# Batch 3's mirrored transform rows from the banks of the others, residual rows gathered and output rows scattered by row number, in a new order

## Chip, core and metric

The kernel runs on one core of one Trainium2 chip. The metric is device time in microseconds of one execution. Engines are named as the profile does: PE (TensorE), DVE (VectorE), ACT (ScalarE), POOL (GpSimd) and SP (SyncE, which here only issues transfers).

## What is computed

A linear-attention recurrence over 768 steps for 4 batches and 8 heads of width 48, then per batch a two-dimensional Fourier mix, a normalisation and a two-layer feed-forward part:

```python
for t in range(S):                      # attention, state is 48 x 48 for each head
    y[:, :, t] = einsum('bhd,bhde->bhe', rt, state + u * kt (x) vt)
    state = wt[:, :, :, None] * state + einsum('bhd,bhe->bhde', kt, vt)
...
X = np.fft.fft(np.fft.fft(x, axis=1), axis=2)      # x: 4 x 768 x 384
u = x + np.real(X)
un = (u - mean(u)) / sqrt(var(u) + 1e-6)            # over the 384 columns
return u + maximum(un @ w_ch1, 0.0) @ w_ch2         # hidden width 1536
```

The real part of the transform of a real array has a symmetry: its value at row 768 - m and column (384 - d) mod 384 is its value at row m, column d.

## The kernel before

**Tiling.** A batch's 768 rows are six chunks (attention) or row blocks (mixing) of 128 rows on 128 partitions. For each chunk, four loads of 192 KB (w, k, r, v) are issued on SP into seven buffers each. The attention of a chunk takes a logarithm of w, two prefix matmuls (lines 773, 777), exponentials on ACT, products on DVE and POOL, two transposes (on PE, or for batch 3 as a DMA transpose on SP, line 819), a score group of sixteen matmuls (line 843), a masking on DVE (line 848), state matmuls (line 869) and the output matmuls (lines 896, 899), whose sum with the direct term becomes `x` (line 908). `fold` then adds and subtracts rows and columns of `x` so that the transforms work on symmetric halves.

**Mixing.** `mix(b)` runs once for each batch. Its steps:
- the row transform, 24 matmuls (line 968) into three banks, evicted to `hcs` (three parts j);
- from `hcs` a reversed copy `hcr` with signs, one operation for each j (lines 977 to 984), since the row blocks 3 to 5 of the transform are a mirror image of blocks 0 to 2;
- for each row block `kb` of six, three matmuls of 384 columns (line 992), against `hcs` for `kb` below 3 and against `hcr` from 3 on, into a bank of its own;
- a DVE sum of that bank with `x` into `uf`, with the row's sum (line 997), a centred copy `un` (line 1000) and a squared sum on ACT (line 1004);
- a transpose of three blocks' `un` into `unt` (for batches 2 and 3 a DMA transpose on SP, line 1033);
- for each half of three row blocks, twelve groups of three matmuls with W1 (line 1056), evicted with a ReLU to `ht` by ACT or DVE (lines 1062, 1064);
- for each row block twelve matmuls with W2 (line 1075, in three parts of four), a DVE operation that scales and adds `uf` into one of three output buffers `osb` (line 1081), and an output store on SP (line 1085). The very last row block is split into 256 and 128 columns.

**Order.** The program is recorded as a list of operations with what each reads and writes. Five hand-kept lists (`ORDER`) give the sequence of operation numbers on each engine. From these `schedule` gives out the eight PSUM banks and adds a few waits between DVE and POOL by a cost model with fixed durations; `emit` puts each engine's operations down in that sequence with the semaphore waits that remain. So the lists decide what stands ahead of what; every engine and SP's queue run in order. The weights are fetched by three transfers on POOL's queue (W1 in two halves, then W2), asked for in the middle of batch 0. Thirty-six filler matmuls (line 1130) stand in PE's list in the first part of the run, and sixteen before it (line 1098).

**Batch 3's end in the old order.** SP issues, after the last loads and the transposes of chunks (3,4) and (3,5), batch 2's outputs, the two `unt` transposes of batch 3 and the last outputs. PE's list runs batch 2's line 1056 and 1075 work between the last attention matmuls and batch 3's transforms.

Of the kernel before, what the change touches and what calls it, by code (L numbers as in the profile page):

```python
# [7 lines left out]
ALU = mybir.AluOpType  # L8
# [28 lines left out]
MEANS = (0, 1, 2, 3)  # L37
# [29 lines left out]
    "act": (  # L67
# [14 lines left out]
    "dve": (  # L82
# [14 lines left out]
    "pool": (  # L97
# [12 lines left out]
}  # L110


class _Tile:


    __slots__ = ("bank", "ops", "pool", "n_done", "end")
# [1047 lines left out]
```

## Time and profile before

| what | value |
|---|---|
| median of three runs | 183.61 us (183.61 to 183.76) |
| profiled execution, its own time | 184.21 us |
| span of that execution in the profile | 182.4 us |
| granted TensorE clock | 1.00 |
| DVE busy | 148.2 us in 341 instructions |
| ACT busy | 130.2 us in 340 |
| POOL busy | 101.5 us in 120 |
| bytes moved by DMA | 28.99 MB, mean 159 GB/s |
| loads of w, k, r and v | 24 each of 192 KB, 3.8 to 4.1 us from issue to landing (median) |

The span is the time between the first and the last instruction that the profile shows; the profiled execution's own time is 1.81 us longer. The page gives each engine's busy time as a share of the span; a chain followed back from the last instruction, from each step to what released it; and groups of instructions by line. Matmuls overlap in the array, so a matmul's own duration (its latency) is about twice what it costs in a row of them.

### The profile page before, as it was taken

The page shows a single profiled execution, that of the slowest core. Times are in us where ns is not written, and L with a number is a line of the kernel's source. Part 1 is how long each engine was busy: PE and PEld are TensorE (multiplying, and loading weights), DVE is VectorE, ACT ScalarE, POOL GpSimd, SP SyncE. Part 2 cuts the span into 40 slices and gives each one's busy share as a digit, 9 for nine tenths or more (in the row PEclk, how much of TensorE's full clock was granted, in tenths as well). Part 3 has the DMA queues.
Part 4 walks back from the last instruction along what each step waited for, and adds up shares of the span by engine and source line. Part 5 has one row for each costly group of instructions (what it writes and reads, how often), then busy time and mean ns, then how long its engine had stood idle before and what let it go on. Part 6 is the DMA issues. An engine that isn't in the chain of part 4 may idle for free.

```text
span 182.4 us, 4568 instructions
## 1 busy us (share of the span) xinstructions
PE 176.8 (97%) x1722; PEld 116.3 (64%) x1722; DVE 148.2 (81%) x341; ACT 130.2 (71%) x340; POOL 101.5 (56%) x120
## 2 busy tenths in 40 slices
PE   7999999999999999999999999999999999999994
PEld 3465676766566666776657666656666676666663
DVE  8779999899899999999888997899979927622343
ACT  2889859597898675799899978888882247478200
POOL 2448789767231498589998968769653440000000
DMA  4999998999999899999999999997550103331214
GB/s 97 203 216 196 208 191 172 185 202 208 152 196 190 162 210 230 226 204 182 202 222 218 219 177 207 220 212 179 103 114 0 47 2 65 73 125 43 86 71 145
DMA packets 116119, 28.99 MB, mean 159 GB/s; under 512 B 111361, under 2 KB 116098, under 8 KB 116098
## 3 DMA queue, kind: packets, MB, share of 16 engines
q1 hardware_dynamic: 114514, 26.36, 70.2%
q0 software_dynamic: 1584, 2.36, 8.0%
q8 instruction: 13, 0.21, 0.5%
q14 instruction: 8, 0.07, 0.1%
HBM read 23.59 MB, written 4.72 MB: 155 GB/s over the span
## 4 chain that ended last, share of the span: by engine, by line
PE 61%; DVE 17%; DMA 9%; SPq 4%; ACT 4%; issue 3%; DVEq 0%
PE bank L1075 18%; PE bank L1056 17%; DMA in_w<-in_w_dram 5%; DMA w<-in_moe_w_ch_dram 4%; DVE ah L848 4%; SPq L609 4%; PE bank L992 3%; PE bank L1130 3%; PE bank L1098 3%; PE bank L968 3%; DVE osb L1081 2%; PE bank L843 2%; DVE rkh L561 2%; PE bank L889 2%; PE bank L899 2%
## 5 line engine op out<-in xcount | busy, mean ns | idle before, releaser
L1075 PE MATMUL bank<-w,ht 128*128 128x384 bf16 (+2 forms) x300 | 53.7, 320 | 0.0
L1056 PE MATMUL bank<-unt,w 128*128 128x384 bf16 x288 | 51.9, 326 | 0.6 <-DMA w<-in_moe_w_ch_dram 0.6
L1064 ACT ACTIVATE ht<-bank 128x384 bf16<-128x384 f32 x72 | 32.6, 496 | 9.3 <-PE bank L1056 8.9
L1056 PEld LDWEIGHTS bank<-unt,w 128*128 128x128 bf16 x288 | 26.9, 98 | 17.5 <-DVE ht L1062 0.8
L1075 PEld LDWEIGHTS bank<-w,ht 128*128 128x128 bf16 x300 | 27.5, 98 | 15.2
L848 DVE TENSOR_TENSOR ah<-bank,msk 128x512 bf16<-128x512 f32 x48 | 31.2, 682 | 2.1 <-PE bank L843 2.0
L561 POOL TENSOR_TENSOR rk<-rk,ub 128x384 f32<-128x384 f32 x21 | 21.6, 1034 | 8.6 <-DVE rk L561 7.0
L561 POOL TENSOR_TENSOR vtd<-in_v,dc 128x384 f32<-128x384 f32 x20 | 16.7, 837 | 11.2 <-DVE dc L800 8.1
L1081 DVE SCALAR_TENSOR_TENSOR osb<-bank,rstd,uf 128x384 f32<-128x384 f32 (+2 forms) x25 | 14.8, 596 | 9.5 <-PE bank L1075 5.9
L1062 DVE TENSOR_SCALAR ht<-bank 128x384 bf16<-128x384 f32 x24 | 13.0, 549 | 6.9 <-PE bank L1056 6.8
L561 POOL TENSOR_TENSOR rk<-in_r,in_k 128x384 f32<-128x384 f32 x17 | 16.9, 999 | 2.9 <-DMA in_r<-in_r_dram 1.4
L997 DVE SCALAR_TENSOR_TENSOR uf<-bank,x 128x384 f32<-128x384 f32 x24 | 12.5, 553 | 4.7 <-PE bank L992 4.6
L561 POOL TENSOR_TENSOR rkh<-in_k,e 128x384 bf16<-128x384 f32 x14 | 14.1, 1009 | 3.6 <-ACT e L792 2.0
L779 ACT ACTIVATE bank<-bank 128x384 f32<-128x384 f32 x24 | 11.5, 484 | 5.8 <-PE bank L773 5.8
L811 DVE TENSOR_TENSOR rkh<-bank,in_r 128x384 bf16<-128x384 f32 x24 | 13.1, 549 | 2.1 <-ACT bank L779 2.0
L575 ACT ACTIVATE xf<-uf,agg 128x384 bf16<-128x384 f32 x24 | 14.7, 614 | 0.0
L561 POOL TENSOR_TENSOR xf<-sd 128x382 bf16<-128x382 f32 (+1 forms) x10 | 10.6, 1062 | 6.5 <-DVE sd L561 3.0
L575 ACT ACTIVATE lb<-in_w 128x384 bf16<-128x384 f32 x24 | 12.4, 519 | 2.1 <-DMA in_w<-in_w_dram 1.8
L575 ACT ACTIVATE un<-uf,agg 128x384 bf16<-128x384 f32 x18 | 10.6, 611 | 4.1 <-DVE uf L997 4.1
L586 ACT ACTIVATE rkt<-bank 128x256 f32<-128x256 f32 x29 | 10.8, 389 | 3.6 <-PE bank L833 2.4
L561 POOL TENSOR_TENSOR sd<-x 128x385 f32<-128x385 f32 x10 | 10.0, 1015 | 5.9 <-DVE x L908 5.4
L792 ACT ACTIVATE e<-bank 128x392 f32<-128x392 f32 (+1 forms) x24 | 11.7, 497 | 2.3 <-DVE bank L877 1.0
(138 smaller groups left out, 358.7 us busy)
## 6 DMA issues: line engine op xcount, KB each, us to landing
in_w<-in_w_dram SPq DMA_DIRECT2D x24, 192.0 KB, 3.8
in_k<-in_k_dram SPq DMA_DIRECT2D x24, 192.0 KB, 3.8
in_r<-in_r_dram SPq DMA_DIRECT2D x24, 192.0 KB, 4.1
in_v<-in_v_dram SPq DMA_DIRECT2D x24, 192.0 KB, 4.0
out_dram<-osb SPq DMA_DIRECT2D x23, 192.0 KB, 2.8
w<-in_moe_w_ch_dram POOLq DMA_DIRECT2D x2, 576.0 KB, 8.1
w<-in_moe_w_ch_dram POOLq DMA_DIRECT2D x1, 1152.0 KB, 10.7
out_dram<-osb SPq DMA_DIRECT2D x1, 128.0 KB, 1.7
```

What stands on the lines that cost most here:

```text
L561: return lambda e: e.tensor_tensor(out=o, in0=a, in1=b, op=f)
L575: return lambda e: e.activation(o, a, f, **kw)
L779: op("act", a_ps(DM) + 20, lambda e: e.activation(ps(tce)[:, 0:DM], ps(tce)[:, 0:DM], ACTF.Exp), w=[tce])
L792: op("act", a_ps(ne), lambda e: e.activation(E2[i2][:, 0:ne], ps(tci)[:, 0:ne], ACTF.Exp), r=[tci], w=[("E2", i2)])
L811: op("dve", v_1(DM), lambda e: e.tensor_tensor(out=rh[:, :, 0:D], in0=ps(tce)[:, 0:DM].rearrange("t (h d) -> t h d", d=D), in1=rt[:, :, :] ...
L848: masked[n] = op("dve", v_1(512), lambda e, x=x: e.tensor_tensor(out=ah[:, x:H:2, :], in0=ps(ta[x])[:, :].rearrange("p (h t) -> p h t", t= ...
L997: op("dve", v_1(DM) + 60, lambda e, kb=kb, t=t: e.scalar_tensor_tensor(out=uf[:, kb, :], in0=ps(t)[:, 0:DM], scalar=1.0, in1=xb[:, kb, 0:D ...
L1056: ins = e.matmul(ps(t)[:, 0:384], W1[:, m, 256 * (j // 2) + j % 2:256 * (j // 2) + 256:2], unt[:, :, m, :], start=(m == 0), stop=(m == NM ...
L1062: {"dve": lambda e, j=j, t=t, ht=ht: e.tensor_scalar(out=ht[:, j, :], in0=ps(t)[:, 0:384], scalar1=su, scalar2=0.0, op0=ALU.mult, op1=ALU. ...
L1064: "act": lambda e, j=j, t=t, ht=ht: e.activation(ht[:, j, :], ps(t)[:, 0:384], ACTF.Relu, scale=su)},
L1075: ins = e.matmul(ps(t)[:, 0:hi - lo], ht[:, j, 128 * x:128 * x + 128], W2[:, j, lo:hi], start=(j == 0), stop=(j == NJ - 1))
L1081: op("dve", v_1(hi - lo) + 64, lambda e, kb=kb, t=t, o=o, lo=lo, hi=hi: e.scalar_tensor_tensor(out=o[:, lo:hi], in0=ps(t)[:, 0:hi - lo], s ...
```

## The change

Batch 3 alone is mirrored (`MIRROR = (3,)`).

- No reversed copy `hcr` is made for batch 3. The banks of row blocks 0, 1 and 2 hold 385 columns instead of 384 (`DTM` has one more column, the first one repeated), and each serves two sums: the plain one for block `kb`, and one that reads the bank's columns 384 to 1 backwards for block `kb + 3`. Row block 3 + q then holds, on partition p, row 768 - (128 q + p), not row 384 + 128 q + p. Row 384 falls on partition 0 of block 3 and gets two matmuls with one output row and a DVE sum on one partition.
- The residual `x` for these rows has to stand on the same partitions. The chunks 3 to 5 of `x` are stored to an internal DRAM tensor by two transfers on SP, and three indirect transfers on POOL's queue gather the rows by number into `uf`.
- The output rows of these blocks are scattered by number: three indirect transfers on POOL's queue take the place of three output stores on SP. The end of the program waits for these too.
- The halves change places: in batch 3 the mirrored half goes first through the feed-forward part's buffers, and the split of the last row block moves to block 2.
- Two small index tables are made on POOL, with two one-element fills.
- The `BST` statistics buffers and the branch that used them, which no batch took, are gone.
- The cost model's load duration changes from 960 to 920 (batch 0) and 1030 (others), and all five lists of `ORDER` are new (left out here).

```diff
-MEANS = (0, 1, 2, 3)
+MIRROR = (3,)
...
-                if o.xfer == 960:
+                if o.xfer in (920, 1030):
...
-                    if s.startswith("out"):
+                    if s[:3] in ("out", "fin"):
...
+    XD = {b: nc.dram_tensor("xd%d" % b, (S // 2, DM), FP32, kind="Internal").ap() for b in MIRROR}
+    RIX = sb("rix", [NP], mybir.dt.uint32)
+    OIX = {b: sb("oix%d" % b, [NP], mybir.dt.uint32) for b in MIRROR}
...
-    DTM = sb("dtm", [3, DM], BF16)
+    DTM = sb("dtm", [3, DM + 2], BF16)
...
+    def move(fn, r, w, sem, xfer):
+        op("sp", 620, fn, r=r, w=w, sem=sem, xfer=xfer, dma=(1150, 600))
...
+    def places():
+        g.ctx = "places"
+        op("pool", 100, lambda e: e.iota(RIX[:, :], [[-128, NP]], base=S // 2, channel_multiplier=-1), w=["RIX"])
+        op(None, {"dve": 60, "pool": 100}, fill(RIX[0:1, 0:1], 0), w=["RIX"])
+        for b in MIRROR:
+            op("pool", 100, lambda e, b=b: e.iota(OIX[b][:, :], [[-128, NP]], base=S * (b + 1), channel_multiplier=-1), w=["OIX%d" % b])
+            op(None, {"dve": 60, "pool": 100}, fill(OIX[b][0:1, 0:1], S * b + S // 2), w=["OIX%d" % b])
...
+            if b in MIRROR:
+                continue
             sg = (1.0, CP[:, :], -1.0)[j]
...
+        if b in MIRROR:
+            xd = XD[b].rearrange("(c p) d -> p c d", p=128)
+            move(lambda e: e.dma_start(xd[:, 0:2, :], xb[:, 3:5, 0:DM]), [("X", i, 3), ("X", i, 4)], [("XD", b, 0)], "xa%d" % i, 1040)
+            move(lambda e: e.dma_start(xd[:, 2, :], xb[:, 5, 0:DM]), [("X", i, 5)], [("XD", b, 1)], "xb%d" % i, 520)
+            for q in (1, 2, 0):
+                op("pool", 1000, lambda e, q=q: e.indirect_dma_start(
+                    uf[:, NP + q, :], None, XD[b], bass.IndirectOffsetOnAxis(ap=RIX[:, q:q + 1], axis=0)),
+                   r=[("XD", b, 0), ("XD", b, 1), "RIX"], w=[("UF", i, NP + q)], sem="xz%d" % q, xfer=520, port=("pool",))
+        for kb in (0, 3, 1, 4, 2, 5) if b in MIRROR else range(NC):
...
+            flip = b in MIRROR and kb >= NP
+            if not flip:
+                t = made[kb] = g.tile("f")
+                for j in range(3):
+                    def f(e, j=j, kb=kb, t=t, w=DM + (b in MIRROR)):
...
+            t = made[kb % NP if flip else kb]
...
+            op("dve", v_1(DM) + 60, lambda e, kb=kb, t=t, flip=flip: e.scalar_tensor_tensor(
+                out=uf[:, kb, :], in0=ps(t)[:, DM:0:-1] if flip else ps(t)[:, 0:DM], scalar=1.0,
+                in1=uf[:, kb, :] if flip else xb[:, kb, 0:DM], op0=ALU.mult, op1=ALU.add,
+                accum_out=agg[:, kb, 0:1]), r=[t, ("UF" if flip else "X", i, kb)], w=[("UF", i, kb), ("SUM", i, kb)])
+            if flip and kb == NP:
...
+                        ins = e.matmul(ps(t)[0:1, 0:DM], hcs[:, j, DM:DM + 1], DTM[:, j, 0:DM], start=(j == 0), stop=(j == 1))
...
-        for hf in range(2):
-            q = 2 * b + hf
+        for hf in ((1, 0) if b in MIRROR else (0, 1)):
+            q = 2 * b + place[hf]
...
-                for lo, hi in ((0, DM),) if n < B * NC - 1 else ((0, 256), (256, DM)):
+                for lo, hi in ((0, DM),) if (b, hf, x) != (B - 1, 0 if b in MIRROR else 1, 2) else ((0, 256), (256, DM)):
...
+                    mq = kb - NP
+                    op("pool", 1000, lambda e, o=o, mq=mq: e.indirect_dma_start(
+                        out.rearrange("b s d -> (b s) d"), bass.IndirectOffsetOnAxis(ap=OIX[b][:, mq:mq + 1], axis=0), o[:, :], None),
+                       r=[("OSB", n % 3, 0), "OIX%d" % b], w=[("out", b, kb, 0)], sem="fin%d" % mq, xfer=520, port=("pool",))
```

In the new lists, PE's last work is row block 1 of batch 3, whole, with block 0 and the parts of the split block 2 just before it; the mirrored half's last part stands 5.9 us of matmuls ahead of the end. SP issues the two stores of `x` right behind the transpose of chunk (3,5), ahead of batch 1's last output. POOL's last six operations are the three gathers and the three scatters. The second half of W1 is asked for on POOL behind a product of chunk (1,2) and, by the wait that the cost model adds, behind DVE's reversed copy of batch 0.

More of the change, by code (lines that the diff above doesn't have):

```diff
@@ L492, in bass_rwkv6_finch__then__fnet_fourier_mix_kernel @@
     UF = [sb("uf%d" % i, [NC, DM], FP32) for i in range(2)]
-    BST = [sb("bst%d" % i, [6], FP32) for i in range(4)]
     AGG = [sb("agg%d" % i, [NC, 2], FP32) for i in range(2)]
@@ L610, in load_one @@
                                                 src[n][b, :, c * CH:(c + 1) * CH, :].rearrange("h t d -> t h d")),
-               w=[("in", n, i)], sem="in_%s%d" % (n, i), xfer=960)
+               w=[("in", n, i)], sem="in_%s%d" % (n, i), xfer=920 if b == 0 else 1030)
         loads[b, c, n] = o
         g.ctx = was
+    def move(fn, r, w, sem, xfer):
+        op("sp", 620, fn, r=r, w=w, sem=sem, xfer=xfer, dma=(1150, 600))
     def small(n, fn, **kw):
@@ L734, in rows @@
                         idn = (IDW if cos or half else NIDW)[p0:p0 + np_, 128 - sh:256 - sh]
-                        src = tab[:, 0:HE] if half == 0 else tab[:, HE - 2:0:-1]
-                        dst = ps(t)[:, 0:HE] if half == 0 else ps(t)[:, HE:DM]
+                        src = tab[:, 0:HE] if half == 0 else tab[:, HE - 2::-1]
+                        dst = ps(t)[:, 0:HE] if half == 0 else ps(t)[:, HE:DM + 1]
                         ins = e.matmul(dst, idn, src, start=(i == 0), stop=(i == len(moves[j]) - 1))
@@ L739, in tables_end @@
             op("pe", 900, rows, r=["IDB", "NIDW"] + [(n, q) for n in ("SS", "CS", "SSl", "CSl") for q in range(2)], w=[t])
-            op("act", a_ps(DM), lambda e, j=j, t=t: e.activation(DTM[:, j, :], ps(t)[:, 0:DM], ACTF.Copy), r=[t], w=["DTM%d" % j])
+            op("act", a_ps(DM), lambda e, j=j, t=t: e.activation(DTM[:, j, 0:DM + 1], ps(t)[:, 0:DM + 1], ACTF.Copy), r=[t], w=["DTM%d" % j])
     def weights():
@@ new lines, in mix @@
+        su = -1.0 / DM
+        made = {}
+        place = {x: 1 - x if b in MIRROR else x for x in range(2)}
+        if b in MIRROR:
[6 more added lines that the diff above has]
+                   r=[("XD", b, 0), ("XD", b, 1), "RIX"], w=[("UF", i, NP + q)], sem="xz%d" % q, xfer=520, port=("pool",))
@@ new lines, in mix, with f @@
+        for kb in (0, 3, 1, 4, 2, 5) if b in MIRROR else range(NC):
+            n = b * NC + kb
+            flip = b in MIRROR and kb >= NP
[3 more added lines that the diff above has]
+                    def f(e, j=j, kb=kb, t=t, w=DM + (b in MIRROR)):
+                        a = 128 * (kb % NP)
+                        return e.matmul(ps(t)[:, 0:w], (hcs if kb < NP else HCR)[:, j, a:a + 128], DTM[:, j, 0:w],
+                                        start=(j == 0), stop=(j == 2))
+                    op("pe", mm(DM), f, r=[("HCS" if kb < NP else "HCR", j), "DTM%d" % j], w=[t])
+            t = made[kb % NP if flip else kb]
+            iu = (2 * b + place[kb // 3]) % len(UN)
+            un = UN[iu][:, kb % 3, :]
+            op("dve", v_1(DM) + 60, lambda e, kb=kb, t=t, flip=flip: e.scalar_tensor_tensor(
[3 more added lines that the diff above has]
+            if flip and kb == NP:
+                t = g.tile("f")
+                def f(e, t=t):
+                    for j in range(2):
+                        ins = e.matmul(ps(t)[0:1, 0:DM], hcs[:, j, DM:DM + 1], DTM[:, j, 0:DM], start=(j == 0), stop=(j == 1))
+                    return ins
+                op("pe", mm(DM, 2), f, r=[("HCS", j) for j in range(2)] + ["DTM%d" % j for j in range(2)], w=[t])
+                op("dve", v_1(DM) + 60, lambda e, kb=kb, t=t: e.scalar_tensor_tensor(
+                    out=uf[0:1, kb, :], in0=ps(t)[0:1, 0:DM], scalar=1.0, in1=xb[0:1, kb, 0:DM], op0=ALU.mult, op1=ALU.add,
+                    accum_out=agg[0:1, kb, 0:1]), r=[t, ("X", i, kb)], w=[("UF", i, kb), ("SUM", i, kb)])
+            op(None, {"act": a_sb(DM) + 95, "dve": v_2(DM) + 60},
+               {"act": act(un, uf[:, kb, :], ACTF.Identity, scale=-float(DM), bias=agg[:, kb, 0:1]),
+                "dve": ts(un, uf[:, kb, :], -float(DM), agg[:, kb, 0:1], ALU.mult, ALU.add)}, port=("dve",),
+               r=[("UF", i, kb), ("SUM", i, kb)], w=[("UN", iu, kb % 3)])
+            op("act", a_sb(DM) + 190, act(xf[:, kb, 63:447], uf[:, kb, :], ACTF.Square, scale=-float(DM), bias=agg[:, kb, 0:1],
+                                          accum_out=agg[:, kb, 1:2]),
+               r=[("UF", i, kb), ("SUM", i, kb)], w=[("AGG", i, kb)] + [(z, i, kb) for z in ("XFe", "XFo", "XFn")])
@@ L1020, in mix @@
             hf = kb // 3
-            unt = UNT[(2 * b + hf) % 2]
+            unt = UNT[(2 * b + place[hf]) % 2]
             if b < DMA_U:
@@ L1030, in mix @@
                 evict(lambda kb=kb, unt=unt: unt[:, kb % 3, :, :].rearrange("p m t -> p (m t)"), lambda tu=tu: psb(tu)[:, 0:DM], DM, 2,
-                      r=[tu], w=[("UNT", (2 * b + hf) % 2, kb % 3)])
+                      r=[tu], w=[("UNT", (2 * b + place[hf]) % 2, kb % 3)])
             elif kb % 3 == 2:
@@ L1034, in mix @@
                     out=unt[:, :, :, :].rearrange("p x m t -> p (x m) t"), in_=UN[iu][:, :, :].rearrange("p x m -> p (x m)")),
-                   r=[("UN", iu, x) for x in range(3)], w=[("UNT", (2 * b + hf) % 2, x) for x in range(3)],
-                   sem="unt%d" % ((2 * b + hf) % 2), xfer=T_XFER, dma=T_LAT)
+                   r=[("UN", iu, x) for x in range(3)], w=[("UNT", (2 * b + place[hf]) % 2, x) for x in range(3)],
+                   sem="unt%d" % ((2 * b + place[hf]) % 2), xfer=T_XFER, dma=T_LAT)
             if kb % 3 == 2:
                 sl = slice(kb - 2, kb + 1)
-                if b in MEANS:
-                    op("act", 187, lambda e, sl=sl: e.activation(lnv[:, sl], agg[:, sl, 1], ACTF.Ln, bias=BEPS[:, :],
-                                                                 scale=float(DM) ** -3),
-                       r=["BEPS"] + [("AGG", i, x) for x in range(kb - 2, kb + 1)], w=[("LNV", i, hf)])
-                else:
-                    op("act", 187, lambda e, sl=sl: e.activation(lnv[:, sl], agg[:, sl, 1], ACTF.Ln, bias=BEPS[:, :]),
-                       r=["BEPS"] + [("AGG", i, x) for x in range(kb - 2, kb + 1)], w=[("LNV", i, hf)])
+                op("act", 187, lambda e, sl=sl: e.activation(lnv[:, sl], agg[:, sl, 1], ACTF.Ln, bias=BEPS[:, :],
+                                                             scale=float(DM) ** -3),
+                   r=["BEPS"] + [("AGG", i, x) for x in range(kb - 2, kb + 1)], w=[("LNV", i, hf)])
                 op("act", 95, lambda e, sl=sl: e.activation(rstd[:, sl], lnv[:, sl], ACTF.Exp, scale=-0.5),
                    r=[("LNV", i, hf)], w=[("RSTD", i, hf)])
-        for hf in range(2):
-            q = 2 * b + hf
+        for hf in ((1, 0) if b in MIRROR else (0, 1)):
+            q = 2 * b + place[hf]
             unt, ht = UNT[q % 2], HT[q % 2]
@@ L1084, in mix @@
                        r=[t, ("RSTD", i, hf), ("UF", i, kb)], w=[("OSB", n % 3, lo)] + ([] if lo else [("OSB", n % 3, 256)]))
-                    op("sp", 620, lambda e, kb=kb, o=o, lo=lo, hi=hi: e.dma_start(
-                        out[b, kb * 128:(kb + 1) * 128, lo:hi], o[:, lo:hi]),
-                       r=[("OSB", n % 3, lo)], w=[("out", b, kb, lo)], sem="out%d" % (n % 3), xfer=520, dma=(1150, 600))
+                    if b not in MIRROR or kb < NP:
+                        move(lambda e, kb=kb, o=o, lo=lo, hi=hi: e.dma_start(out[b, kb * 128:(kb + 1) * 128, lo:hi], o[:, lo:hi]),
+                             [("OSB", n % 3, lo)], [("out", b, kb, lo)], "out%d" % (n % 3), 520)
+                        continue
+                    mq = kb - NP
+                    op("pool", 1000, lambda e, o=o, mq=mq: e.indirect_dma_start(
+                        out.rearrange("b s d -> (b s) d"), bass.IndirectOffsetOnAxis(ap=OIX[b][:, mq:mq + 1], axis=0), o[:, :], None),
+                       r=[("OSB", n % 3, 0), "OIX%d" % b], w=[("out", b, kb, 0)], sem="fin%d" % mq, xfer=520, port=("pool",))
     g.ctx = "begin"
@@ L1103, in bass_rwkv6_finch__then__fnet_fourier_mix_kernel @@
     masks()
+    places()
     fills()
```

32 lines of the change are left out of this document (removed), and 128 rows, old and new, of the table ORDER.

## The prediction

> **What bounds the kernel now.** I read the page first, then who TensorE (PE) waited for, busy time by stretch, and the chain that ended last.
>
> ```profile
> span 182.4 us, 4568 instructions
> ...
> PE 61%; DVE 17%; DMA 9%; SPq 4%; ACT 4%; issue 3%; DVEq 0%
> ```
>
> PE carries most of the chain that set the end. The waits of PE (who waited for whom, us in total, times, longest) are few:
>
> ```profile
> PE bank L1098 <- DVE w L572: 1.3, 1, 1.3
> PE bank L1056 <- DMA w<-in_moe_w_ch_dram: 0.6, 1, 0.6
> PE bank L777 <- ACT ht L1064: 0.3, 1, 0.3
> PE bank L833 <- POOL rkh L561: 0.3, 1, 0.3
> PE bank L843 <- ACT ht L1064: 0.2, 1, 0.2
> ```
>
> These are all of them, 2.7 us. By stretch (its bounds and length, busy us and count of PE, PEld, DVE, ACT, POOL, then granted clock, DMA share, GB/s):
>
> ```profile
> 45.00:112.00 67.00, 65.89 (x735) 44.90 (x734) 63.05 (x129) 57.56 (x162) 47.40 (x51) 1.00 1.03 200
> 112.00:150.00 38.00, 37.84 (x350) 24.74 (x348) 31.18 (x68) 25.23 (x65) 23.73 (x26) 1.00 0.54 116
> 150.00:180.00 30.00, 29.81 (x196) 18.46 (x193) 13.57 (x33) 13.80 (x38) 0.34 (x1) 1.00 0.28 81
> ```
>
> Up to 112 us the loads keep the DMA engines full (share 1.03) and VectorE (DVE) is busy 63 of 67 us: PE, DVE and DMA are all near their limit. After 112 us the DMA share falls to 0.54 and 0.28 and only PE stays full. The chain agrees (start us, us, what):
>
> ```profile
> 37.82 8.02 DMA w<-in_moe_w_ch_dram
> 45.97 1.14 PE bank L1056 x6
> ...
> 112.59 0.40 PE bank L843 x8
> ...
> 136.87 0.55 PE bank L843 x16
> ...
> 156.38 7.80 PE bank L1056 x48
> ...
> 173.28 6.54 PE bank L1075 x52
> ...
> 179.92 0.35 DVE osb L1081
> ```
>
> From 112.59 us to 179.82 (173.28 + 6.54), the end of PE's work, the chain is PE and nothing else. In it 48 matmuls of 384 columns take 7.80 us, 0.1625 us each: my unit below. A score group (sixteen matmuls of line 843) takes 0.55 us.
>
> Is PE short of time before 112 us too? At 45.97 it starts the first matmul that needs the second half of W1. Counted in those two units, the matmuls that stand behind that point in the old order make about 131 us; the clock to 179.82 shows 133.9. So about 3 us of hidden gaps lie between 46 and 112 us, and there are the fillers (line 1130, 36 in either order) and the start before that. A new order can win back at most these; what it can lose has no such bound.
>
> **The change part by part.** On PE, batch 3's mixing loses nine matmuls that read the reversed copy `hcr` and gains two for row 384. In batch 3 what touches that copy is (smallest, median, largest ns, then first and last start):
>
> ```profile
> L992 PE MATMUL bank<-dtm,hcr x9: 326/326/326, 150.9 to 153.5; 128*128 128x384 bf16 x9
> L978 ACT ACTIVATE hcr<-hcs x2: 507/512/516, 149.3 to 151.0; 128x384 bf16<-128x384 bf16 x2
> L565 POOL TENSOR_SCALAR hcr<-hcs,cp x1: 1250/1250/1250, 149.1 to 149.1; 128x384 bf16<-128x384 bf16 x1
> ```
>
> The 326 ns is the latency of one; in a pipelined row it costs 0.1625 us. PE saves 7 x 0.1625 = 1.14 us, in a stretch where PE alone sets the end. The three copies (0.51, 0.51 and 1.25 us) go too, but they ran beside matmuls of line 1075 while PE never waited: worth nothing; were PE to run dry there, one copy's 0.51 us would be the gain. Widening the other matmuls by one column is 0.4 ns each: nothing.
>
> The end gets longer. The old order's last PE work is the 128-column part of the split last row block. In the new order the split block is x = 2 of the unmirrored half, but the last PE work is x = 1 of that half, unsplit: 384 columns to evict and 192 KB to store after PE's end. The rows for both sizes:
>
> ```profile
> 178.38 0.62 DVE L1081 SCALAR_TENSOR_TENSOR osb<-bank,rstd,uf 128x384 f32<-128x384 f32 x1 [0.68 <-PE bank L1075]
> ...
> 179.92 0.35 DVE L1081 SCALAR_TENSOR_TENSOR osb<-bank,rstd,uf 128x128 f32<-128x128 f32 x1 [0.19 <-PE bank L1075]
> ```
>
> ```profile
> out_dram<-osb SPq DMA_DIRECT2D x1, 192.0 KB, 1.9
> ...
> out_dram<-osb SPq DMA_DIRECT2D x1, 64.0 KB, 1.6
> ```
>
> That is 0.62 - 0.35 = 0.27 us on DVE and 1.9 - 1.6 = 0.3 us on the store, 0.57 us that nothing hides.
>
> The residual's way through DRAM (two stores on SP, three gathers on POOL) is new. It lies beside matmuls, so it costs nothing if it is in time. I count back from PE's end E by the matmuls behind each point in the new order. The attention products of chunks (3,4) and (3,5) have changed places: (3,5)'s now comes first and ends 40.3 us before E. These rows price the steps:
>
> ```profile
> 142.57 0.54 DVE L908 TENSOR_TENSOR x<-bank,vtd 128x384 f32<-128x384 f32 x1
> ...
> 149.92 0.56 DVE L997 SCALAR_TENSOR_TENSOR uf<-bank,x 128x384 f32<-128x384 f32 x1 [3.46 <-PE bank L992]
> ```
>
> ```profile
> w<-in_moe_w_ch_dram POOLq DMA_DIRECT2D x2, 576.0 KB, 8.1
> w<-in_moe_w_ch_dram POOLq DMA_DIRECT2D x1, 1152.0 KB, 10.7
> ```
>
> ```profile
> 37.82 0.80 POOL L745 DMA_DIRECT2D w<-in_moe_w_ch_dram  x1 [0.73 <-DVE rkh L561]
> 38.88 0.99 POOL L561 TENSOR_TENSOR rk<-in_r,in_k 128x384 f32<-128x384 f32 x1 [0.26 <-DVE hcr L565]
> ```
>
> ```profile
> unt<-un SPq DMA_TRANSPOSE x4, 3.3
> ```
>
> X of (3,5) is ready at E-39.6 (0.54 and a handover). The store, priced at the 1.9 us of an output store, lands by about E-37.3. Nothing in the trace is an indirect DMA. Its issue I take at 0.8 us, as POOL's weight DMA. Its landing is bounded by 1.9 us (192 KB from SP) and 10.7 us (1152 KB on POOL's queue, among loads); I take 3, near the low end, since its size is the former's and the DMA share there is 0.28 to 0.54. Issued at E-37.3, -36.5 and -35.7, the last lands at E-32.7. DVE comes to the first flipped sum only at about E-28.3: PE ends row block 0 at E-29.6, then follow DVE's sum of it (0.56) and an output eviction (0.62). So there are 4 us in hand. The three flipped sums and the one for row 384 end at about E-26.1, `un` at E-25.4, and its transpose (3.3 us) at E-22.1; PE needs it at E-20.5. The margin of the whole path is 1.6 us, and a gather must take 9 to 10 us before it fails. At the high bound of 10.7 us the sums start 2.6 us late and PE loses 1.0 us there.
>
> SP's queue holds, behind the second store of X, batch 1's last output, the transpose of the unmirrored half and two of batch 2's outputs; an output that waits there only holds its buffer, and batch 2 needs that buffer later, at E-27. The transpose is needed at E-24.1; its last `un` comes from row block 0, so it is asked at about E-28.2 and lands at E-24.9, 0.8 us in hand.
>
> The three scatters replace SP's outputs. The mirrored half comes first, its last row block leaves PE at E-5.9, is evicted at E-5.2 and issued on POOL, which has nothing else to do. It would have to take 8 us to land after the last plain output (E+2.7). At 10.7 us it would cost about 2.8 us; I take nothing.
>
> The index set-up (two iotas, two fills) is under 0.5 us on POOL and DVE in a start that has fillers on PE: nothing.
>
> The new order as such is the large unknown. Every queue changes. I found one place where the old order had PE wait on a transfer: the second half of W1, asked at 37.82 and needed 8.02 us later. The old order lets POOL ask for it behind a DVE product of chunk (1,2), the new one behind DVE's reversed copy in batch 0, which in the old order released POOL's next product only at 38.88. Behind the same first product of chunk (1,0), the new order has three operations ahead of that copy, the old one five. Bounds of the order's effect: the 3 us of hidden gaps gained, or a comparable amount lost; I take 0, since the amount of PE work ahead of that point differs by only 0.2 us in the two orders.
>
> Sum: -1.14 + 0.57 = -0.57 us. On the profiled span of 182.4 us that is 181.8; the profiled execution took 184.21 us, 1.81 around its span, so 183.64; the median shown is 0.60 under that execution: 183.04, given as 183.0.
>
> **The rivals.** (a) The second half of W1 comes later, and the kernel is slower. Place: POOL's ask in batch 0. For it: PE already waits 0.6 us there, so each us of delay goes through to the end, and DVE, which has to reach the copy first, is busy 63 of the next 67 us. Against: the copy has fewer operations ahead of it now. It decides as soon as the ask comes after 37.82; a copy at its old place gives 38.88 - 37.82 = 1.1 us: 183.04 + 1.1 = 184.1.
>
> (b) The gathers or scatters are late, as priced at the high bound: 183.04 + 1.0 to 2.8, middle 184.9. For it: POOL's queue shows 8.1 and 10.7 us. Against: those were larger transfers among loads.
>
> The Trainium skill, in SBUF — State Buffer, section "SBUF: two separate sides", says that a DMA issued from GpSimd has its descriptors written through a port that VectorE's two-port modes lock; this rule would make the late gathers of (b) likelier wherever DVE runs such an instruction beside them. By it the time would be that of (b), without it that of the forecast; no run so far shows an indirect DMA, so the trace does not decide it.
>
> (c) The new order also closes half of the hidden gaps: 183.04 - 1.5 = 181.5. For it: with DMA at 1.03 and DVE at 94% there, the order of loads matters. Against: the gaps are only 3 us in 66.
>
> **How the numbers follow.** Forecast 0.45, with its own range 182.5 to 183.6; (a) 0.25; (b) 0.10; (c) 0.20. A measurement of this kernel can tell about 0.2%, 0.37 us, from no change: faster is below 183.24, slower above 183.98. Of the forecast's 0.45, 0.28 lies below 183.24, 0.15 within and 0.02 above. So faster 0.28 + 0.20 = 0.48, same 0.15, slower 0.02 + 0.25 + 0.10 = 0.37. The range of 8 in 10 takes in most of (c) and of (a) and (b): 181.7 to 185.2.
>
> **What would show it.** Right: PE without a gap in the chain from about 112 us on, no wait of PE for `unt` of batch 3; the nine matmuls gone; span minus PE's end about 3.1 us where it was 2.6; gathers landing in about 3 us. Wrong: a wait of PE or of DVE on a gather, or a last landing from POOL's queue after SP's (b); a wait of PE for `w` well over 0.6 us (a); first transform matmuls of batch 3, seen from PE's end, where they stood, but PE's end more than 2 us earlier (c).

## The result and the profile after

The changed kernel takes 182.18 us (median of 20 runs), beside 183.61 us for the kernel before on the same chip (20 runs). The ratio is 0.9936 with an interval of 0.9913 to 0.9958: 1.2 us faster, from 0.8 to 1.6. It is taken without the slow executions of both kernels, so 1.2 us is not the difference of the two medians. The forecast was 0.57 us faster. A second comparison on another chip gave 0.9921 (0.9887 to 0.9956). The direction was right and the gain is about twice as large. The profiled execution took 182.78 us for a span of 181.0; before it was 184.21 and 182.4.

Read in the order of the prediction. First all waits of PE in the changed kernel (who waited for whom, us in total, times, longest):

```profile
PE bank L1126 <- DVE w L574: 1.3, 1, 1.3
PE bank L912 <- DVE ah L861: 1.3, 1, 1.3
PE bank L1159 <- DVE idw L567: 0.2, 1, 0.2
PE bank L902 <- POOL vtd L563: 0.2, 1, 0.2
PE bank L840 <- DVE rkh L824: 0.2, 1, 0.2
PE bank L882 <- ACT e L805: 0.2, 1, 0.2
```

No wait for `unt` and, in this execution, none for `w` from DRAM. By stretch, with the columns as before:

```profile
45.00:112.00 67.00, 67.00 (x747) 45.74 (x746) 63.13 (x133) 58.19 (x163) 44.45 (x48) 1.00 0.97 198
112.00:150.00 38.00, 38.00 (x352) 24.34 (x350) 34.05 (x75) 26.20 (x66) 27.01 (x28) 1.00 0.66 141
150.00:180.00 30.00, 27.85 (x184) 17.21 (x181) 15.42 (x33) 9.18 (x27) 2.97 (x3) 1.00 0.32 99
```

From 45 to 112 us PE is now busy in all 67.00 us, with 747 matmuls; before it was 65.89 and 735. So in this pair of profiles the change gained where the forecast had put a zero. In the last stretch PE is busy without a break up to its end at 177.7. The chain and VectorE (DVE) at the end:

```profile
165.63 3.25 PE bank L1098 x20
169.37 7.84 PE bank L1098 x60
```

```profile
174.41 0.48 DVE L1104 SCALAR_TENSOR_TENSOR osb<-bank,rstd,uf 128x256 f32<-128x256 f32 x1 [1.26 <-PE bank L1098]
176.66 0.35 DVE L1104 SCALAR_TENSOR_TENSOR osb<-bank,rstd,uf 128x128 f32<-128x128 f32 x1 [1.76 <-PE bank L1098]
177.31 1.27 DVE L1104 SCALAR_TENSOR_TENSOR osb<-bank,rstd,uf 128x384 f32<-128x384 f32 x2 [0.30 <-PE bank L1098]
```

The two small pieces of the split block are evicted first, and two full ones follow, as the diff showed. For the new way through DRAM, POOL's own instructions first (the first gather waits for the stores of x), and then transfers (count, KB each, median us to landing):

```profile
144.11 1.12 POOL L1008 DMA_INDIRECT uf<-xd,rix  x1 [1.94 <-DMA xd<-x]
145.53 0.97 POOL L1008 DMA_INDIRECT uf<-xd,rix  x1 [0.31 <-issue]
146.81 0.95 POOL L1008 DMA_INDIRECT uf<-xd,rix  x1 [0.30 <-issue]
...
173.62 0.97 POOL L1113 DMA_INDIRECT out_dram<-osb,oix  x1 [0.30 <-issue]
```

```profile
xd<-x SPq DMA_DIRECT2D x1, 384.0 KB, 3.0
xd<-x SPq DMA_DIRECT2D x1, 192.0 KB, 3.0
...
uf<-xd,rix POOLq DMA_INDIRECT x3, 3.1
out_dram<-osb,oix POOLq DMA_INDIRECT x3, 2.6
```

To split the 1.4 us between the two spans I add up PE's gaps: the time from the start of one matmul to the start of the next, less the price of the first when they follow one another (in the trace 162 ns for 384 columns, 83 for 193, 55 for 128; I use columns/2.4 + 2.5 ns for all wider ones, and for those of 48 columns and fewer what they take in a row). Only differences between rows are read. PE's end is the start of its last matmul plus its price; the span is taken to a hundredth. The table holds all profiles that the following sections use, in us.

| kernel | PE's end | span less PE's end | gaps to 40 | 40 to 110 | from 110 | all gaps |
|---|---|---|---|---|---|---|
| before | 179.65 | 2.73 | 1.96 | 3.36 | 1.12 | 6.44 |
| before again | 181.52 | 2.73 | 1.97 | 4.34 | 2.01 | 8.32 |
| changed | 177.68 | 3.28 | 3.09 | 1.39 | 1.13 | 5.61 |
| changed again | 177.73 | 3.28 | 1.99 | 2.51 | 1.15 | 5.65 |
| order alone | 178.85 | 3.28 | 3.04 | 1.68 | 0.92 | 5.64 |
| seven back | 179.38 | 3.28 | 2.11 | 2.82 | 1.22 | 6.15 |
| split last | 178.32 | 2.92 | 2.84 | 2.27 | 1.13 | 6.24 |
| k first | 177.30 | 3.29 | 1.83 | 2.28 | 1.11 | 5.22 |
| both | 178.77 | 2.93 | 2.39 | 3.14 | 1.15 | 6.68 |
| fewer fillers | 178.54 | 3.29 | 4.82 | 2.86 | 1.36 | 9.04 |
| gathers late, 3 memsets | 177.53 | 3.28 | 2.50 | 1.76 | 1.18 | 5.44 |
| gathers late, 9 memsets | 182.80 | 3.28 | 2.06 | 2.33 | 6.30 | 10.69 |
| no wait, first profile | 185.39 | 3.28 | 2.73 | 9.29 | 1.29 | 13.31 |
| no wait, again | 177.69 | 3.28 | 1.83 | 2.51 | 1.27 | 5.61 |

Between the first and the third row PE's end moved by -1.97: -1.14 for seven matmuls and -0.83 for gaps. What follows PE's end grew by 0.55. The sum is -1.42; the spans differ by 1.41 (182.38 and 180.97).

### The profile page after: what moved, and what is told of

The parts are those of the page before. It is cut to its first block, busy times and chain, and to the rows that moved or that the text cites. A ratio compares the mean times of both kernels' runs of the same rounds, so it can differ in the third digit from the quotient of the medians.

```text
span 181.0 us, 4586 instructions
## 1 busy us (share of the span) xinstructions
PE 174.3 (96%) x1715; PEld 114.3 (63%) x1715; DVE 151.6 (84%) x357; ACT 126.9 (70%) x330; POOL 102.9 (57%) x123
## 4 chain that ended last, share of the span: by engine, by line
PE 85%; SPq 6%; DMA 3%; DVE 2%; POOL 1%; issue 1%; DVEq 0%; POOLq 0%
PE bank L1079 26%; PE bank L1098 26%; SPq L611 6%; PE bank L1019 6%; PE bank L981 5%; PE bank L856 4%; DMA in_k<-in_k_dram 3%; PE bank L912 2%; PE bank L909 2%; PE bank L786 2%; PE bank L840 2%; PE bank L846 2%; PE bank L790 2%; PE bank L882 2%; PE bank L902 1%; PE bank L1159 1%
## 5 line engine op out<-in xcount | busy, mean ns | idle before, releaser
L1079 PE MATMUL bank<-unt,w 128*128 128x384 bf16 x288 | 53.5, 326 | 0.0
L1087 ACT ACTIVATE ht<-bank 128x384 bf16<-128x384 f32 x67 | 30.9, 492 | 10.8 <-PE bank L1079 10.8
L563 POOL TENSOR_TENSOR rkh<-in_k,e 128x384 bf16<-128x384 f32 x17 | 17.2, 1011 | 11.7 <-ACT e L805 10.4
L563 POOL TENSOR_TENSOR vtd<-in_v,dc 128x384 f32<-128x384 f32 x22 | 18.2, 832 | 7.5 <-DVE dc L813 5.5
L1085 DVE TENSOR_SCALAR ht<-bank 128x384 bf16<-128x384 f32 x29 | 15.4, 552 | 5.8 <-PE bank L1079 5.5
L1113 POOL DMA_INDIRECT out_dram<-osb,oix x3 | 3.0, 991 | 23.9 <-DVE osb L1104 23.3
L577 ACT ACTIVATE un<-uf,agg 128x384 bf16<-128x384 f32 x21 | 12.1, 607 | 4.6 <-DVE uf L1025 4.5
L813 DVE TENSOR_REDUCE dc<-rk 128x8 f32<-128x384 f32 x24 | 13.0, 543 | 0.2 <-POOL rk L563 0.2
L563 POOL TENSOR_TENSOR xf<-sd 128x384 bf16<-128x384 f32 (+1 forms) x8 | 8.6, 1086 | 7.0 <-DVE sd L563 3.9
L912 PE MATMUL bank<-vb,ah 128*128 128x48 bf16 x192 | 11.3, 183 | 1.3 <-DVE ah L861 1.3
```

Source lines behind the costliest of these rows:

```text
L563: return lambda e: e.tensor_tensor(out=o, in0=a, in1=b, op=f)
L577: return lambda e: e.activation(o, a, f, **kw)
L813: op("dve", v_1(DM), lambda e: e.tensor_reduce(out=dc[:, :], in_=rku[:, :, :], axis=mybir.AxisListType.X, op=ALU.add), r=[("RK", i2)], w=[ ...
L912: ins = e.matmul(ps(ty)[:, D * h:D * h + D], ah[:, h, :], vb[:, h, :], start=first and not ype, stop=True, skip_group_check=True)
L1079: ins = e.matmul(ps(t)[:, 0:384], W1[:, m, 256 * (j // 2) + j % 2:256 * (j // 2) + 256:2], unt[:, :, m, :], start=(m == 0), stop=(m == NM ...
L1085: {"dve": lambda e, j=j, t=t, ht=ht: e.tensor_scalar(out=ht[:, j, :], in0=ps(t)[:, 0:384], scalar1=su, scalar2=0.0, op0=ALU.mult, op1=ALU. ...
```

## The experiments

**The order without the mirror.** Is the gain the matmuls' or the order's? The mirror is switched off; order, half order and split stay those of the changed kernel, and the nine matmuls stand from the place of row 384's two on, three at a time. The five lists are numbered anew for it (left out here).

```
-MIRROR = (3,)
+MIRROR = ()
...
-        place = {x: 1 - x if b in MIRROR else x for x in range(2)}
+        place = {x: 1 - x if b == 3 else x for x in range(2)}
...
-        for hf in ((1, 0) if b in MIRROR else (0, 1)):
+        for hf in ((1, 0) if b == 3 else (0, 1)):
...
-                for lo, hi in ((0, DM),) if (b, hf, x) != (B - 1, 0 if b in MIRROR else 1, 2) else ((0, 256), (256, DM)):
+                for lo, hi in ((0, DM),) if (b, hf, x) != (B - 1, 0, 2) else ((0, 256), (256, DM)):
```

> The changed kernel's order on all engines, its halves of batch 3 in the changed order and its unsplit last block, but without mirroring: the three reversed copies and the nine matmuls of 384 columns are back, the residual rows are read where they lie, the output rows go out by plain stores. Theory (the trace of the changed kernel: PE ended 1.96 us earlier, seven matmuls are 1.14 of it, the rest fewer gaps from the order; the end is 0.56 longer): PE ends 1.14 later than in the changed kernel, near 178.9, the end after it stays about 3.1, time 183.2 to 183.4, 0.2 to 0.4 under the kernel before. Rival, the prediction's zero for the order: time is that of the kernel before plus 0.57, 184.2. Rival, that all of the gain is the order's: 182.2, as the changed kernel.

The chain of the changed kernel and then that of the order alone, in the last feed-forward stage of batch 3:

```profile
154.91 10.72 PE bank L1079 x66
...
169.37 7.84 PE bank L1098 x60
```

```profile
156.07 10.72 PE bank L1079 x66
...
170.54 7.84 PE bank L1098 x60
```

The same 66 matmuls start 1.16 us later, PE ends 1.17 later and all gaps differ by only 0.03: what the mirror wins is the 1.14 of its seven matmuls. The time was 184.47 us beside 185.3 for the kernel before on this chip, ratio 0.9952 (0.9923 to 0.9981), 0.9 us faster although what follows PE's end is longer by 0.55. The time forecast for a neutral order, slower by 0.57, lies outside.

**Seven matmuls back.** The same question from the other side: seven more matmuls into the bank of row 384, result not used.

```
                 def f(e, t=t):
+                    for j in range(7):
+                        e.matmul(ps(t)[:, 0:DM], MSK[:, :], IDW[:, :])
                     for j in range(2):
```

> The changed kernel with seven more matmuls of 384 columns (product not used) ahead of the two that make row 384. Theory: PE has no wait from 112 us on, so each costs its 0.1625 us: PE ends 1.14 later, time +1.1 to +1.2 against the changed kernel. Rival: the matmuls that the mirror takes away lay beside waits for the transposed halves; PE's end moves by less than 0.4.

PE ended 1.70 us later. Of that 1.14 is the matmuls, 0.54 other gaps; only 0.09 of these lie behind 110 us, where the matmuls were put. That stretch has nothing to hide work behind. The ratio to the kernel before, 0.9998 (0.9934 to 1.0061), is too wide to add to it, so the price rests on the profile.

**The two kernels again.** One profile each is thin ground for a statement on an order.

> The changed kernel as it is, beside the three others on one chip. Theory: PE's gaps (start of one matmul to the next, less its columns over 2.4 per ns and 2.5 ns) sum to 5.2 to 6.2 us, as in five profiles of that order; the time stands 1.0 to 1.6 under the kernel before. Rival: the 0.8 us that the order seemed to win was one lucky profile; the time stands 0.57 under it, as forecast.

> The kernel before as it is, for a second profile. Theory (the order wins): its gaps sum to 6.2 to 6.9 us again, with PE waiting on W1's half near 46 us and on an eviction near 93. Rival (run to run): 5.2 to 6.0, inside what the changed order shows.

Changed again: ratio 0.9921, all gaps 5.65. The kernel before showed 8.32 in its second profile, more than either expectation, but from an execution of 186.06 us, 1.8% above the fastest of that kernel on the chip and above its median of 184.81. Its longest waits:

```profile
PE bank L1098 <- DVE w L572: 1.3, 1, 1.3
PE bank L843 <- DMA rkt<-rkh: 0.9, 1, 0.9
PE bank L833 <- DVE rkh L561: 0.8, 1, 0.8
PE bank L1056 <- DMA w<-in_moe_w_ch_dram: 0.7, 1, 0.7
PE bank L1075 <- DMA w<-in_moe_w_ch_dram: 0.5, 1, 0.5
```

The waits at the start and for W1's half (line 1056) are there again, the other three are new. The stretch from 45 to 112 us in the second profile of each, before and then changed:

```profile
45.00:112.00 67.00, 64.76 (x723) 44.11 (x721) 61.54 (x128) 57.20 (x161) 46.68 (x51) 1.00 1.00 194
```

```profile
45.00:112.00 67.00, 66.41 (x738) 45.07 (x735) 63.17 (x130) 57.59 (x159) 44.34 (x48) 1.00 0.98 196
```

Nine of the table's profiles have the changed order, all fillers and no delay that reaches PE (left out are fewer fillers, nine memsets and the first of no wait). Their gaps are 5.2 to 6.7 us in all, 5.8 in the mean; the two of the old order have 6.4 and 8.3. They overlap, so the profiles alone don't size the order: the lower of the two gives 0.6 us, and the higher, which would give 2.5, comes from that long execution. The times say more. Less the 0.59 that the matmuls and the longer end make together, the result gives 1.2 - 0.59 = 0.6 us (0.2 to 1.0) and the second comparison 0.9 (0.2 to 1.5); the order alone gives 0.9 + 0.55 = 1.4 (0.9 to 2.0).

**The split block last.** Is the end's price what the prediction read off the rows? The split block's second part goes last on PE, DVE and SP.

```
 "pe"  ... -1408 1393 1403 1409 1404 1405 1398 1399 1394 1410 1395 1400
           +1393 1403 1404 1405 1398 1399 1394 1395 1400 1408 1409 1410
 "dve" ... -1406 1411 1396 1401   +1406 1396 1401 1411
 "sp"  ... -1407 1412 1397 1402   +1407 1397 1402 1412
```

> The changed kernel, but the block whose output is split into 256 and 128 columns comes last on PE, DVE and SP. Theory: what lies behind PE's end is set by the last block's size (DVE 0.62 against 0.35 us, and the 192 KB store against 64 KB); the end falls from 3.14 to about 2.6, time 181.6, PE's end unchanged at 177.8. Rival: three stores asked within 2 us share the engines and the last one is no faster; no change, 182.2.

Behind PE's end came 2.92 us, not 3.28: 0.36 of the 0.55 is won back. DVE's last three evictions now run in one piece and end at 178.94:

```profile
177.27 1.67 DVE L1103 SCALAR_TENSOR_TENSOR osb<-bank,rstd,uf 128x384 f32<-128x384 f32 x3 [2.18 <-PE bank L1097]
```

That is 0.62 behind PE's end, as in the kernel before (180.27 after 179.65), where the changed kernel had 0.89. The 0.19 left over lies behind DVE, with the store of 64 KB: 2.30 us to the span's end, before 2.11. So that much of the rival, three stores in quick succession, may be true.

PE's end was 0.63 later than in the changed kernel, all of it gaps ahead of 110 us, where nothing was edited; it was expected unchanged. The ratio to the kernel before was 0.9871 (0.983 to 0.9912); set against the order alone on the same chip that is 1.5 us, beside 1.14 + 0.36 = 1.50 from the traces.

**k of chunk 3 ahead of r.** In the changed kernel's first profile PE waits 1.3 us at 19 us for `ah`, since DVE stands before it waiting for a load:

```profile
17.95 0.56 DVE L563 TENSOR_TENSOR rkh<-in_k,e 128x384 bf16<-128x384 f32 x1 [2.02 <-DMA in_k<-in_k_dram]
```

The edit is one swap in SP's order, `87 86` to `86 87`.

> The changed kernel with one swap on SP: the load of k of chunk 3 (asked at 12.57 us) goes ahead of that of r of the same chunk (asked at 11.40 us). Theory: DVE's wait of 2.02 us at 17.95 and PE's gap of 1.47 us behind it come from that landing; it comes about 1.1 us earlier, PE's gap falls to about 0.4, PE ends about 1 us earlier, time about 181.1. Rival: the loads take turns on full DMA engines and r is then late by as much, so the gap only moves to the next chunk's work: within 0.3 us of the changed kernel. Second rival: PE's start gains, and waits behind it (W1's half, softmax factors) take it back between 40 and 110 us: gaps there rise from 1.39 by the amount won.

> The changed kernel with the split block last and the load of k of chunk 3 ahead of that of r. Theory: the two gains add, 0.44 at the end (2.88 against 3.32 between PE's last matmul and the span's end) and 0.3 to 1.2 at the start; time 0.7 to 1.6 under the changed kernel on the same chip, about 2 under the kernel before. Rival: PE's gap at 19 us comes and goes from run to run (a run with the same order up to there did not have it), so the swap gives nothing: 0.4 to 0.5 under the changed kernel.

With the swap the wait is gone, gaps to 40 us are 1.83 and 2.39; PE ended 0.4 us earlier with the swap alone, not the 1 expected, and the ratio to the kernel before was 0.9893 (0.9846 to 0.994). But without the swap DVE waited there 1.62 us in split last, 0.55 with three memsets, and not at all in changed again, seven back and no wait again. So the landing varies from one execution to the next, and the swap's gain is not shown. Both edits together, expected 0.4 to 1.6 us under the changed kernel, took 182.93 us beside 182.75 for the changed kernel in the same comparison, ratios 0.9915 (0.988 to 0.995) and 0.9921 to the kernel before: not told apart. The shorter end is there (2.93), the time doesn't resolve it.

**Fewer fillers.**

```
-    NW = 36
+    NW = 20
```

> The changed kernel with 20 filler matmuls in place of 36; the last 16 (from about 14 to 40 us) are left out. Theory: fillers stand where PE would wait anyway; PE's end moves by less than 0.3 us. Rival: behind each stands work that is ready, PE wins 0.16 us for each, up to 2.6 us in all. Second rival: without them the granted clock falls in the first 50 us, and the time grows by over 1 us.

Sixteen matmuls less are 2.60 us, and the gaps rose by 3.43: PE ended 0.86 later, not earlier, where less than 0.3 was expected. Ahead of 40 us, where the fillers had stood, the gaps rose by 1.73, so about two thirds of their time stood in waits. Another 1.47 came between 40 and 110 us, where the two profiles of the changed kernel already differ by 1.12 (1.39 and 2.51). The ratio to the kernel before, 0.9926 (0.9892 to 0.9959), is not told apart from that of the changed kernel, and the granted clock stayed at 0.997 over the span. PE's gaps before 40 us are therefore no measure of what a start costs as long as the number of fillers differs.

**Nothing waits for the gathers.** They land in a dead input buffer.

```
-                    uf[:, NP + q, :], None, XD[b], ...
+                    INB["w"][q][:, :, :].rearrange("p h d -> p (h d)"), None, XD[b], ...
-                in1=uf[:, kb, :] if flip else xb[:, kb, 0:DM], op0=ALU.mult, op1=ALU.add,
+                in1=xb[:, kb, 0:DM], op0=ALU.mult, op1=ALU.add,
```

> The changed kernel, but the three gathers land in a dead input buffer and the flipped sums add the unpermuted rows of x (so the residual of the mirrored half is not the reference's): nothing waits for a gather. Theory: the gathers are hidden; PE's end stays within 0.2 us of 177.8. Rival: they hold the flipped sums at 149 us and PE behind them: PE ends 0.5 us or more earlier.

The first profile is of use only behind 110 us. A load of r came 5.7 us late in another batch:

```profile
60.00 0.56 DVE L563 TENSOR_TENSOR rk<-in_r,in_k 128x384 f32<-128x384 f32 x1 [5.70 <-DMA in_r<-in_r_dram]
```

> The kernel in which nothing waits for the gathers (the residual of the mirrored half is not the reference's), profiled once more, since a load of r came 5 us late in its first profile. Theory: the gathers are hidden with nothing to spare at the sums and about 1.5 us at the transposed half; PE ends within 0.4 us of the changed kernel's 177.7, no wait of PE from 112 us on in either. Rival: PE ends 0.5 us or more earlier.

Again: PE's end 177.69 beside 177.68, gaps from 110 us 1.27 beside 1.13; the ratio to the kernel before was 0.9931 (0.989 to 0.9972), that of the changed kernel in the same comparison 0.9921. The gathers cost nothing.

**Gathers later.** How near are they to costing something? Memsets on POOL, in buffers that are no longer used, by the code ahead of the second gather. In POOL's order that one (q = 2) comes first, so they delay all three.

```
+            def gather(e, q):
+                for x in range(3 if q == 2 else 0):      # 9 in the second
+                    e.memset(HCR[:, x, :] if x < 3 else INB["k"][x - 3][:, :, :].rearrange("p h d -> p (h d)"), 0.0)
...
```

The delay is less than the memsets' time, since the first of them begins at 143.42 us, as soon as the stores have landed, where the changed kernel's first gather begins only at 144.11: the last gather is asked at 147.42 and at 149.75 us, after 146.81.

> The changed kernel with three memsets of 384 columns on POOL between the first and the second gather, estimated at 0.4 us each: two gathers about 1.2 us later. Prediction's account (4 us in hand before the first flipped sum, 1.6 us to the transposed half): no change. The trace of the changed kernel (last gather lands near 149.9, sums at 149.4 to 150.8, the transposed half lands about 1.2 us before its first use): DVE's sums wait about 1 us, PE moves by 0 to 0.3.

> The same with nine memsets, about 3.7 us. Prediction's account (4 us in hand): PE moves by less than 0.2. The trace of the changed kernel (no slack at the sums, about 1.2 us at the transposed half): the sums go about 3.7 us later, PE waits for the transposed half and ends about 2.5 us later.

With 0.61 us more, DVE waits 0.61 at the second flipped sum (first line; the two below are of the longer delay):

```profile
150.43 0.56 DVE L1029 SCALAR_TENSOR_TENSOR uf<-bank,uf 128x384 f32<-128x384 f32 x1 [0.61 <-DMA uf<-xd,rix]
```

```profile
151.75 0.56 DVE L1029 SCALAR_TENSOR_TENSOR uf<-bank,uf 128x384 f32<-128x384 f32 x1 [2.29 <-DMA uf<-xd,rix]
...
154.25 0.56 DVE L1029 SCALAR_TENSOR_TENSOR uf<-bank,uf 128x384 f32<-128x384 f32 x1 [1.94 <-DMA uf<-xd,rix]
```

So DVE had nothing in hand at that sum, and PE had: it ended within 0.2 us of the changed kernel. The changed kernel itself shows the same in its second profile, where the last gather was asked at 147.34 and DVE waited 0.48 there. With the longer delay the last gather, asked 2.94 later, held DVE to 154.25, 4.5 us after its request where it took 3.0 with the shorter one; the transpose of `un` that was asked beside it, at 149.35, took 4.7 where it took 3.2, so the two seem to have shared the engines. The other transpose, asked alone, took 3.2. The transpose of the mirrored half was asked 4.43 later (157.24 after 152.81). PE's matmuls before and behind that wait, and the stretches around it (the granted clock is the third number from the end):

```profile
155.29 2.60 PE L1083 MATMUL bank<-unt,w 128*128 128x384 bf16 x15
160.62 7.69 PE L1083 MATMUL bank<-unt,w 128*128 128x384 bf16 x36 [2.72 <-DMA unt<-un]
```

```profile
155.00:160.00 5.00, 2.89 (x18) 1.48 (x16) 4.53 (x12) 5.00 (x16) 0.00 (x0) 1.00 0.34 69
160.00:162.00 2.00, 1.39 (x7) 0.82 (x8) 0.56 (x1) 0.50 (x2) 0.00 (x0) 0.85 0.50 180
162.00:164.00 2.00, 2.00 (x7) 0.91 (x6) 0.56 (x1) 0.00 (x0) 0.00 (x0) 0.50 0.00 0
164.00:166.00 2.00, 2.00 (x11) 1.14 (x10) 0.58 (x2) 0.00 (x0) 0.00 (x0) 0.80 0.00 0
```

PE ended 5.1 us later, twice the 2.5 expected. Two waits for `unt` of 3.1 us together make 3.4 from start to start; about 1.7 more were lost since PE's clock was granted at half from 161.40 to 164.81 us, 3.41 us long: there its matmuls of 384 columns start 0.32 us apart.

## Why the prediction was right, and where its sizes were off

**What bounds the kernel: right.** From 112 us on PE is the end's only cause in the changed kernel as well (38.00 of 38.00 us), shown by seven matmuls that cost their full price both when taken away and when put back (gaps elsewhere set apart).

**Seven matmuls, -1.14: right** (order alone: 1.17, of which 0.03 gaps). The three reversed copies were rightly counted as nothing: PE's end moved by no more than the matmuls.

**The longer end, +0.57: right** (2.73 to 3.28, +0.55), and in its parts: DVE's end moved from 0.62 to 0.89 behind PE's, the 0.27 that was reckoned, and the store's part from 2.11 to 2.40, 0.29 where it was 0.3.

**The order, 0: this is the term that was mis-sized.** The prediction named its room, about 3 us of hidden gaps from 46 us to the end, and took zero as the middle between gain and loss, with half of the gaps as rival (c). In the first pair of profiles the gaps from 40 to 110 us fell from 3.36 to 1.39 and those before rose by 1.13, in all -0.83; the three comparisons of times say -0.6, -0.9 and -1.4. So the truth most likely lies between the forecast and (c), whose sign, PE's end more than 2 us earlier, was just missed with 1.97. That the sum came out within range is in part luck, since a term without a known sign had been put at nothing. Which of the many moves does it was not settled: no single wait of the old order accounts for it. In the two profiles of the old order the wait for W1's half makes 0.6 to 0.7 us; the rest are waits of 0.2 to 0.9 us on other operations, which change from one profile to the next.

**Rival (a), W1's half: its condition came true in some profiles, its price did not.** In the first profile of the changed kernel POOL asked for it 1.04 us later than before, behind DVE's reversed copy as feared:

```profile
38.86 0.83 POOL L758 DMA_DIRECT2D w<-in_moe_w_ch_dram  x1 [0.43 <-DVE hcr L567]
```

The transfer then took 7.2 us where it had taken 8.0 and landed at 46.02, 0.2 later than before, and PE, which had lost 1.13 us more in gaps ahead of 40 us, was not there earlier. In the second profile POOL asked at 37.75, no later than before (37.82), the half landed at 45.31, and PE waited 0.2 us; in the first profile of "no wait" it asked at 38.49 and PE waited 0.7, as long as in the old order. So the time of the request changes from one execution to the next by as much as the rival feared from the order. The prediction carried each us of delay through to PE; that needs the transfer to take as long as before and PE to arrive when it did.

**The way through DRAM, hidden: right, with less in hand than worked out.** Against "4 us in hand" at the first flipped sums there was nothing. Counted back from PE's end E = 177.7, x of chunk (3,5) was ready at E-37.9 (139.78) where E-39.6 was reckoned; from there to the first gather it took 4.33 us, not 2.3 (the stores, one behind the other on SP, landed in 3.0 each, not the 1.9 of an output store, and the gather began 0.9 after the landing); from the first gather to the third 2.70, not 1.6, since each takes 0.95 to 1.12 on POOL and 0.3 in between, not 0.8. Together 1.7 + 2.0 + 1.1 = 4.8. The landing taken at 3 us was 3.1. "The margin of the whole path is 1.6 us" held: 4.43 us of delay made PE wait 2.72. So the step that failed is the lead at the sums, and the step behind it, which decides, was right; "a gather must take 9 to 10 us before it fails" falls with the former, as from 3 us on each 1 us more is taken from those 1.6. That the sums began on time all the same was luck: the whole lead was used up, and in the second profile 0.5 us more than that.

**Rival (b)** did not occur. Its rule, from the Trainium skill (SBUF — State Buffer, section "SBUF: two separate sides"), that a DVE mode with two ports keeps POOL from writing descriptors, was not put to the test: between 144 and 150 us, where the gathers were issued, DVE ran casts, sums and scalings out of banks only, and each indirect DMA held POOL for 0.95 to 1.12 us. Its price was too low on one count: with a wait of PE near 3 us, 1.7 us more went with the clock. The scatters cost nothing, as reckoned: the last is asked at 173.62 and lands 2.6 later, ahead of the last plain outputs.

## What to carry to other kernels

Removed work is worth its full price where one engine is busy almost throughout (here 37.84 of 38.00 us before the change), and such a stretch can be proved by putting the same work back. An order that changes as a whole shouldn't be entered as zero because its sign is unknown: where PE idles in many waits of 0.2 to 0.9 us that differ between executions, look at several profiles of the old order before sizing what a new one can win, and size it by repeated times rather than by one pair of profiles. When a new chain is placed beside other work, say which step has slack and which decides; here the early step had none and cost nothing, as 1.6 us stood behind it.

## What the runs showed of the hardware

- A PE wait of 2.72 us, ahead of which PE had started matmuls without a gap since 154.16 us, brought the granted clock to 0.50 (7 matmuls of 384 columns in 162 to 164 us, where 12 fit). The clock fell 0.8 us after PE had resumed, at 161.40, and stayed there for 3.41 us, so the wait cost 1.7 us more than its length. After the 5.4 us wait in the first profile of "no wait" the clock was 0.54 in the mean from 60 to 65 us. The Trainium skill (TensorE: Matmul & The Clock Gate, section "Part 1: The HAM clock gate (the "warmup" mystery)") gives half clock after at least an idle window of about 3.4 us; here a wait shorter than that was enough. The waits of at most 1.3 us elsewhere did not lower it (0.997 to 1.0 over the span in the profiles without a longer one).
- An indirect DMA of 128 rows of 1.5 KB holds POOL for 0.95 to 1.12 us, the next follows after 0.3, a gather lands in 3.1 and a scatter in 2.6. A 192 KB store to a DRAM buffer took 3.0 us to land where the last outputs of that size took 1.9.
- Loads of one and the same order land differently: DVE waited 2.02, 1.62 or 0 us for k at 18 us, and once 5.70 us for r at 60 us.
